# Shifting the rescaled high words in SBUF, and a second PSUM buffer for the early attention of a fused attention and feed-forward kernel

## Chip, cores and metric

One core of one Trainium2 chip runs the whole program. The metric is the device time of one execution in microseconds; the kernel before takes 642.7 us (median of 3 runs, 642.09 to 643.06).

## What is computed

The reference is chunked attention (batch 4, 8 heads, 768 positions of width 64; each chunk of 32 queries sees 16 keys to its left, itself, 8 to its right and 8 memory keys), whose output, 3072 tokens of width 512, goes through a feed-forward layer with a rational activation. The weights `w_in` and `w_out` come as float64.

```
scores = scale * q_c @ k_full.T;  a = exp(scores - max);  a = a / (sum(a) + 1e-9);  out_c = a @ v_full
x = out.reshape(3072, 512);  h = x @ w_in                                  # 512 x 2048
P = a0 + a1*h + a2*h^2 + a3*h^3;  Q = 1 + |b0|*|h| + |b1|*h^2
g = P / (Q + 1e-6);  result = g @ w_out                                     # 2048 x 512
```

## The kernel before, in words

The tokens form 8 blocks of 384. A block needs 4 units of attention (two heads each) and then 16 steps, one for each slice of 128 columns of `w_in`: 128 steps in all. In a step TensorE (PE) makes `h` with 12 matmuls (`g1`, L397), the activation chain turns `h` into `g` on ScalarE (ACT), VectorE (DVE) and GpSimd (POOL) (`chain_...`, L448 to L491), and a step or two later 9 matmuls add `g @ w_out` into three PSUM banks (`g2`, L412). Each operand is split into a high and a low float32r part, so every product is three matmuls.

A unit of attention is scores (`att_scores`, L274, PE), maximum and subtraction (`att_max`, L282 to L295, DVE), exponential (L300, ACT), transposes (`att_turn`, L315, PE), a copy (`att_keep`, L322, ACT), values (`att_values`, L331, PE), division (`att_norm`, L339 to L349, DVE), transposes back (`att_back`, L360, PE) and the split into `x_hi` and `x_lo` (L364 to L377). Scores, transposes, values and transposes back each take a fresh PSUM tile from `pa()` (L249 to L256).

The 32 halves of the weight slices are converted from float64 bits on the chip, each 128x512 words, in five steps: load the pair of 32-bit words to `w_raw` in SBUF (SP queue, L117); `w_abs` (L165, ACT) rescales the high word, read at a step of two words, with Prelu into a PSUM tile `stage`; `w_bits` (DVE) shifts `stage` left by 3 in place (L170) and ors it to the low word shifted right by 29 (L171), back into the low words of `w_raw`; `w_hi` (L179, ACT) rounds to the high part and `w_lo` (L184, POOL) subtracts it.

The first 30 steps, their attention and all conversions stand in an order written out by hand, the table `SEQ` (tokens `A`, `B`, `H`, `L` are `w_abs`, `w_bits`, `w_hi`, `w_lo`; `b01` is the scores of block 0, unit 1, `g` and `o` are `g1` and `g2`, `r` is `chain_ratio`). Each engine runs its instructions strictly in that order, and so does the SP queue with the loads. From step 30 on a loop sets the order, and `stage` is no longer used.

PSUM has 8 banks here: three for `o`, two for `h`, one for `cr` (the chain's reciprocal), and two in `ps_a`. While `SEQ` runs, the two of `ps_a` have the tags `pa0` and `pa1`, one buffer each: attention of blocks 1 and 2 always uses `pa0`; `stage` alternates between both for the first 6 conversions (`STAGE2`) and then uses `pa1`. Block 0 uses the banks of `o` and `cr`.

Of the kernel before, what the change touches and what calls it, by code (L numbers as in the profile page):

```python
# [12 lines left out]
F32 = mybir.dt.float32  # L13
F32R = mybir.dt.float32r
U32 = mybir.dt.uint32
AF = mybir.ActivationFunctionType
ALU = mybir.AluOpType
# [7 lines left out]
F64_REBIAS = 2.0 ** -111  # L25
SIGN_STEP = 2.0 ** 32
# [14 lines left out]
STAGE2 = 6  # L41
# [24 lines left out]
def attn_moe(ctx, tc, qk, vm, w, a, b, out):  # L66
    nc = tc.nc
    P = 128
    NBLK, NPAIR = qk.shape[:2]
    NJT, DM = w.shape[0], out.shape[1]  # L70
# [18 lines left out]
    ps_h = ctx.enter_context(tc.tile_pool(name="ps_h", bufs=2, space=bass.MemoryType.PSUM))  # L89
    ps_r = ctx.enter_context(tc.tile_pool(name="ps_r", bufs=1, space=bass.MemoryType.PSUM))  # L90
    hand_pool = ExitStack()
    ps_a = hand_pool.enter_context(tc.tile_pool(name="ps_a", bufs=1, space=bass.MemoryType.PSUM))

    nc.scalar.preload_act_table_set("natural_log_exp_and_others")

# [16 lines left out]
    def pin(ins):  # L112
        if pinned[0]:
            tc.keep_in_program_order(ins)
# [7 lines left out]
    conv, raws, split = {}, {}, {}  # L122
# [29 lines left out]
    def words(key):  # L152
        t = half(raws[key[1]], key[0]).rearrange("p (f two) -> p f two", two=2)
        return t[:, :, 0], t[:, :, 1]
# [6 lines left out]

    def w_abs(key):
        low, high = words(key)
        f = conv[key] = ps_a.tile([P, DM], F32, name="stage", tag=f"pa{int(done['A'] >= STAGE2 or done['A'] % 2)}")
        pin(nc.scalar.activation(f, high.bitcast(F32), AF.Prelu, scale=F64_REBIAS, alpha=-SIGN_STEP))  # L165

    def w_bits(key):
        low, high = words(key)
        fi = conv.pop(key).bitcast(U32)
        pin(nc.vector.tensor_scalar(fi, fi, 3, None, op0=ALU.logical_shift_left))  # L170
        pin(nc.vector.scalar_tensor_tensor(low, low, 29, fi, op0=ALU.logical_shift_right, op1=ALU.bitwise_or))  # L171

    def w_hi(key):
        kind, j = key
# [73 lines left out]
    turn, ring = [0], [False]  # L248

    def pa(i):  # L250
        turn[0] = (turn[0] + 1) % 4
        if i == 0:
            if turn[0] == 3:
                return ps_r.tile([P, 512], F32, name="pa", tag="cr")
            return ps_o.tile([P, DM], F32, name="pa", tag=f"o{turn[0]}")
        return ps_a.tile([P, 512], F32, name="pa", tag="pa" if ring[0] else "pa0")  # L256

    def places(i):
        return [(g, j, 4 * g + j if i < BLOCKWISE else NG * j + g) for g in range(NG) for j in range(4)]
# [8 lines left out]
    def att_scores(i, p):  # L268
        u = unit[i, p]
        users[qk_slot(i, p)] = users.get(qk_slot(i, p), 0) - 1  # L270
        s = u["s"] = pa(i)
        sv = s[:, :NG * 2 * KEYS].rearrange("x (g h w) -> x g h w", g=NG, h=2)
        for g, j, c in places(i):
            pin(nc.tensor.matmul(sv[j * CHUNK:(j + 1) * CHUNK, g], lhsT=u["q"][c],  # L274
                                 rhs=u["k"][c], start=True, stop=True, tile_position=(0, j * CHUNK)))
# [31 lines left out]
    def att_turn(i, p):  # L307
        u = unit[i, p]
        if i >= BLOCKWISE:
            u["eT"] = across(turn_blocks(u.pop("e").rearrange("x g w h -> x g (w h)")), "eT")  # L310
            return
        ep = u["ep"] = pa(i)
        e = u.pop("e")
        for g in range(NG):
            pin(nc.tensor.transpose(out=ep[:, g * P:(g + 1) * P], in_=e[:, g], identity=ident))  # L315
# [8 lines left out]
    def att_values(i, p):  # L324
        u = unit[i, p]
        if i == 0 and p >= 2:
            users[V_SLOTS[p - 2]] -= 1
        o = u["o"] = pa(i)
        ov = o[:, :NG * 2 * (D + 1)].rearrange("x (g h d) -> x g h d", g=NG, h=2)
        for g, j, c in places(i):  # L330
            pin(nc.tensor.matmul(ov[j * CHUNK:(j + 1) * CHUNK, g],  # L331
                                 lhsT=u["eT"][:, c * CHUNK:(c + 1) * CHUNK], rhs=u["v"][c],
                                 start=True, stop=True, tile_position=(0, j * CHUNK)))
# [166 lines left out]
    done = dict.fromkeys("wABHL", 0)  # L500
# [61 lines left out]

    single = dict(g=g1, s=chain_abs, p=chain_below, i=chain_line, j=chain_above, t=chain_inverse, r=chain_ratio, u=chain_hi, y=chain_lo, o=g2)
    convert = dict(w=lambda key: w_load(*key), A=w_abs, B=w_bits, H=w_hi, L=w_lo)

    def hand(token):
# [28 lines left out]
    ps_a = ctx.enter_context(tc.tile_pool(name="ps_b", bufs=2, space=bass.MemoryType.PSUM))  # L595
# [90 lines left out]
```

## Time and profile before

| what | value |
|---|---|
| time, median of 3 runs | 642.7 us (642.09 to 643.06) |
| profiled execution: span from first to last instruction | 641.9 us |
| around the span, against the median | 0.8 us |
| TensorE busy | 615.4 us, 96% |
| VectorE busy | 500.8 us, 78% |
| ScalarE busy | 432.7 us, 67% |
| GpSimd busy | 431.7 us, 67% |
| mean granted TensorE clock | 0.981 |

The trace has no time of its own for the execution beside its span, so the span stands for it; the lowest run (642.09) is 0.2 us above it. The table averages over stages with different limits: the slices of the page show TensorE near full from the fourth slice on, and all conversions lie in the first 178 us.

### The profile page before, as it was taken

The numbers are of one execution on the slowest core, as the hardware profiler recorded it, in microseconds if no ns is written. First come the engines' busy times: TensorE is split into PE (matmuls) and PEld (weight loads), VectorE is DVE, ScalarE is ACT, GpSimd is POOL, SyncE is SP. The second block draws the span as 40 slices with busy tenths as digits, with TensorE's granted clock in tenths as the row PEclk, the third lists the DMA queues.
The fourth block names the chain that finished last, engine by engine and source line by source line (L and its number), as shares of the span: only waits on it lengthen the run. The fifth ranks groups of instructions, "written<-read, shape, count | busy, mean of one in ns | idle before, by whom it ended". The sixth has DMA issues, their size and how long they took to land.

```text
span 641.9 us, 12300 instructions
## 1 busy us (share of the span) xinstructions
PE 615.4 (96%) x4312; PEld 537.7 (84%) x4312; DVE 500.8 (78%) x1001; ACT 432.7 (67%) x814; POOL 431.7 (67%) x457
## 2 busy tenths in 40 slices
PE   4769999999999999999999999999999999999997
PEld 3567787889988888888898888888988888999995
DVE  5777998997967878888787777887877787666665
ACT  4567787877965566665666766676666766676664
POOL 5457775868885656766666666676666666777762
PEclk8778999999999999999999999999999999999999
DMA  7998127403212385424322433214223310000001
GB/s 250 348 384 304 64 63 240 160 1 112 96 62 87 85 267 164 147 79 126 95 77 80 137 87 87 66 50 129 76 80 87 100 26 13 13 34 17 1 1 50
DMA packets 43566, 69.69 MB, mean 109 GB/s; under 512 B 26480, under 2 KB 26480, under 8 KB 43120
## 3 DMA queue, kind: packets, MB, share of 16 engines
q1 hardware_dynamic: 42256, 64.17, 31.5%
q10 hardware_dynamic: 960, 3.16, 1.5%
q0 software_dynamic: 288, 1.57, 0.8%
q8 instruction: 34, 0.56, 0.4%
q14 instruction: 28, 0.23, 0.1%
HBM read 51.58 MB, written 9.44 MB: 95 GB/s over the span
## 4 chain that ended last, share of the span: by engine, by line
PE 55%; issue 15%; POOL 13%; DVE 8%; DMA 4%; ACT 4%; SPq 1%; POOLq 0%; DVEq 0%; ACTq 0%
PE h L397 25%; PE o L412 23%; POOL glo L491 5%; POOL ghi L484 5%; PE pa L274 3%; PE pa L331 3%; DMA qk<-in_qk_dram 2%; DMA w_raw<-in_w_dram 2%; DVE stage L170 1%; DVE ct L477 1%; POOL cy L458 1%; DVE w_raw L171 1%; DVE cr L478 1%; DVE ct L479 1%; SPq L117 1%
## 5 line engine op out<-in xcount | busy, mean ns | idle before, releaser
L397 PE MATMUL h<-x_hi,w_hl 128*128 128x384 f32 x1024 | 268.5, 343 | 3.3 <-DVE ct L468 3.2
L412 PE MATMUL o<-w_hl,ghi 128*128 128x512 f32 x768 | 240.1, 393 | 0.3 <-ACT ghi L486 0.3
L458 POOL TENSOR_TENSOR cy<-cy,ha 128x384 f32<-128x384 f32 x128 | 130.3, 1018 | 148.4 <-ACT cy L454 146.1
L397 PEld LDWEIGHTS h<-x_hi,w_hl 128*128 128x128 f32 x1024 | 187.3, 190 | 17.3 <-issue 5.8
L397 PE MATMUL h<-x_lo,w_hl 128*128 128x384 f32 x512 | 173.8, 339 | 0.0
L412 PEld LDWEIGHTS o<-w_hl,ghi 128*128 128x128 f32 x768 | 141.5, 188 | 21.6 <-issue 1.0
L412 PE MATMUL o<-w_hl,glo 128*128 128x512 f32 x384 | 151.4, 394 | 0.4 <-POOL glo L491 0.2
L491 POOL TENSOR_TENSOR glo<-ct,ghi 128x384 fp32r<-128x384 f32 x126 | 127.9, 1015 | 9.1
L453 ACT ACTIVATE ha<-h 128x384 f32<-128x384 f32 x128 | 62.9, 492 | 100.9 <-PE h L397 96.2
L467 DVE TENSOR_TENSOR ct<-ct,h 128x384 f32<-128x384 f32 x128 | 70.1, 547 | 61.5 <-ACT ct L463 61.5
L484 POOL TENSOR_TENSOR ghi<-ct,zero 128x384 fp32r<-128x384 f32 x126 | 104.6, 830 | 9.8 <-DVE ct L479 7.3
L477 DVE SCALAR_TENSOR_TENSOR ct<-ct,par,cr 128x384 f32<-128x384 f32 x128 | 78.4, 612 | 37.1 <-ACT cr L473 34.0
L472 ACT ACTIVATE cr<-cy 128x384 f32<-128x384 f32 x128 | 63.3, 494 | 57.4 <-POOL cy L458 52.4
L397 PEld LDWEIGHTS h<-x_lo,w_hl 128*128 128x128 f32 x512 | 97.2, 190 | 0.0
L454 ACT ACTIVATE cy<-ha,bab 128x384 f32<-128x384 f32 x128 | 90.8, 710 | 4.2
L412 PEld LDWEIGHTS o<-w_hl,glo 128*128 128x128 f32 x384 | 72.0, 187 | 21.5 <-POOL glo L491 1.2
L463 ACT ACTIVATE ct<-h,par 128x384 f32<-128x384 f32 x128 | 84.0, 657 | 0.0
L468 DVE SCALAR_TENSOR_TENSOR ct<-ct,par,h 128x384 f32<-128x384 f32 x128 | 78.7, 615 | 4.5
L479 DVE SCALAR_TENSOR_TENSOR ct<-cr,ct 128x384 f32<-128x384 f32 x128 | 71.3, 557 | 4.4
L478 DVE SCALAR_TENSOR_TENSOR cr<-cy,cr 128x384 f32<-128x384 f32 x128 | 71.0, 555 | 0.4
L473 ACT ACTIVATE cr<-cr 128x384 f32<-128x384 f32 x128 | 60.8, 475 | 4.0
L184 POOL TENSOR_TENSOR w_hl<-w_raw,w_hl 128x512 fp32r<-128x512 f32 x32 | 42.0, 1311 | 26.0 <-ACT w_hl L179 25.0
(60 smaller groups left out, 419.9 us busy)
## 6 DMA issues: line engine op xcount, KB each, us to landing
qk<-in_qk_dram SPq DMA_DIRECT2D x56, 288.0 KB, 3.4
w_raw<-in_w_dram SPq DMA_DIRECT2D x26, 512.0 KB, 7.5
v_main<-in_vm_dram SPq DMA_DIRECT2D x56, 195.0 KB, 3.9
out_dram<-stage SPq DMA_DIRECT2D x24, 256.0 KB, 3.3
eT<-blocks SPq DMA_DIRECT2D x80, 48.0 KB, 2.0
xf<-blocks SPq DMA_DIRECT2D x80, 48.0 KB, 2.0
w_raw<-in_w_dram SPq DMA_DIRECT2D x3, 1024.0 KB, 4.7
qk<-in_qk_dram ACTq DMA_DIRECT2D x8, 288.0 KB, 3.6
```

Source lines behind the costliest of these rows:

```text
L397: pin(nc.tensor.matmul(h[:, :TB], lhsT=wt[:, cols], rhs=xt[i][:, ct, :], start=m == 0, stop=m == last))
L412: ins = nc.tensor.matmul(o, lhsT=gt[:, cols], rhs=wt, start=begin and m == 0, stop=end and m == 2)
L454: pin(nc.scalar.activation(c["y"], c["ha"], AF.Identity, scale=B1, bias=B0))
L458: pin(nc.gpsimd.tensor_tensor(c["y"], c["y"], c.pop("ha"), op=ALU.mult))
L463: pin(nc.scalar.activation(c["t"], c["h"], AF.Identity, scale=A3, bias=A2))
L467: pin(nc.vector.tensor_tensor(t, t, h, op=ALU.mult))
L468: pin(nc.vector.scalar_tensor_tensor(t, t, A1, h, op0=ALU.add, op1=ALU.mult))
L477: pin(nc.vector.scalar_tensor_tensor(t, t, A0, r, op0=ALU.add, op1=ALU.mult))
L478: pin(nc.vector.scalar_tensor_tensor(r, yy, QC, r, op0=ALU.add, op1=ALU.mult))
L479: pin(nc.vector.scalar_tensor_tensor(t, r, 2.0, t, op0=ALU.subtract, op1=ALU.mult, reverse0=True))
L484: pin(nc.gpsimd.tensor_tensor(ghi, chain[z]["t"], zero.broadcast_to([P, TB]), op=ALU.add))
L491: pin(engine.tensor_tensor(glo, chain.pop(z)["t"], gh[z].bitcast(F32), op=ALU.subtract))
```

## The change

`w_abs` writes the rescaled high word back to where it read it, in SBUF. `w_bits` shifts it there, and the or takes both of its inputs from SBUF. No `stage` tile is left, so `ps_a` becomes one tag `pa` with two buffers, and attention of blocks 1 and 2 in the first 30 steps alternates between two banks. Below the edit all lines move up by one.

```diff
-    ps_a = hand_pool.enter_context(tc.tile_pool(name="ps_a", bufs=1, space=bass.MemoryType.PSUM))
+    ps_a = hand_pool.enter_context(tc.tile_pool(name="ps_a", bufs=2, space=bass.MemoryType.PSUM))
...
     def w_abs(key):
         low, high = words(key)
-        f = conv[key] = ps_a.tile([P, DM], F32, name="stage", tag=f"pa{int(done['A'] >= STAGE2 or done['A'] % 2)}")
-        pin(nc.scalar.activation(f, high.bitcast(F32), AF.Prelu, scale=F64_REBIAS, alpha=-SIGN_STEP))
+        high = high.bitcast(F32)
+        pin(nc.scalar.activation(high, high, AF.Prelu, scale=F64_REBIAS, alpha=-SIGN_STEP))
 
     def w_bits(key):
         low, high = words(key)
-        fi = conv.pop(key).bitcast(U32)
-        pin(nc.vector.tensor_scalar(fi, fi, 3, None, op0=ALU.logical_shift_left))
-        pin(nc.vector.scalar_tensor_tensor(low, low, 29, fi, op0=ALU.logical_shift_right, op1=ALU.bitwise_or))
+        pin(nc.vector.tensor_scalar(high, high, 3, None, op0=ALU.logical_shift_left))
+        pin(nc.vector.scalar_tensor_tensor(low, low, 29, high, op0=ALU.logical_shift_right, op1=ALU.bitwise_or))
...
-        return ps_a.tile([P, 512], F32, name="pa", tag="pa" if ring[0] else "pa0")
+        return ps_a.tile([P, 512], F32, name="pa", tag="pa")
```

On PE, DVE, ACT and POOL the same instructions stand in the same order as before; what differs is their operands and what they wait for. On DVE, the first two conversions between steps of the chain (`w_raw` is the loaded weights, `stage` the PSUM tile, `ct` and `cr` tiles of the chain), before:

```order
L468 SCALAR_TENSOR_TENSOR ct<-ct,par,h 128x384 [waits DVE_49]
L170 TENSOR_SCALAR stage<-stage 128x512 [waits Activation_49]
L171 SCALAR_TENSOR_TENSOR w_raw<-w_raw,stage 128x512 [waits DMAHW1_49,DMAHW5_49,DVE_49,Pool_49]
L477 SCALAR_TENSOR_TENSOR ct<-ct,par,cr 128x384
L478 SCALAR_TENSOR_TENSOR cr<-cy,cr 128x384 [waits Pool_49]
```

and of the change:

```order
L467 SCALAR_TENSOR_TENSOR ct<-ct,par,h 128x384 [waits DVE_49]
L169 TENSOR_SCALAR w_raw<-w_raw 128x512 [waits DMAHW1_49,DMAHW5_49,Activation_49,Pool_49]
L170 SCALAR_TENSOR_TENSOR w_raw<-w_raw 128x512 [waits DVE_49]
L476 SCALAR_TENSOR_TENSOR ct<-ct,par,cr 128x384
L477 SCALAR_TENSOR_TENSOR cr<-cy,cr 128x384 [waits Pool_49]
```

Nothing moved; both instructions of a conversion now work on `w_raw` in SBUF alone.

On PE, the scores of the first two units of block 1 (`pa` is the attention's PSUM tile), ahead of the first step's `h`, before:

```order
L274 MATMUL pa<-qk 32x128 [waits DMAHW2_49,DMAHW1_49,DVE_49]
L360 MATMUL pa<-ident,xt 128x128 [waits DVE_49,Activation_49]
L274 MATMUL pa<-qk 32x128 [waits DMAHW5_49,DMAHW6_49,DVE_49,PE_49]
L397 MATMUL h<-x_hi_102,w_hl 128x384
...
L315 MATMUL pa<-ident,e 128x128 [waits DVE_49,PE_49]
```

and of the change:

```order
L273 MATMUL pa<-qk 32x128 [waits DMAHW2_49,DMAHW1_49]
L359 MATMUL pa<-ident,xt 128x128 [waits DVE_49,Activation_49]
L273 MATMUL pa<-qk 32x128 [waits DMAHW6_49,DMAHW5_49]
L396 MATMUL h<-x_hi_102,w_hl 128x384
...
L314 MATMUL pa<-ident,e 128x128 [waits PE_49]
```

The waits on DVE for a free bank are gone from these three.

On the SP queue one pair of loads of values (`v_main`, two of 195 KB) moves ahead of two loads of weights:

```order
 L117 DMA v_main_101<-in_vm_dram 64x780 x2
 L117 DMA w_raw<-in_w_dram 128x1024 x2
-L117 DMA w_raw<-in_w_dram 128x2048 x2
+L117 DMA w_raw<-in_w_dram 128x2048
+L117 DMA v_main_101<-in_vm_dram 64x780 x2
+L117 DMA w_raw<-in_w_dram 128x2048
 L117 DMA part_109<-spare 128x512 x3
 L117 DMA w_raw<-in_w_dram 128x2048
-L117 DMA v_main_101<-in_vm_dram 64x780 x2
 L117 DMA qk<-in_qk_dram 64x1152 x2
```

The second whole-slice load of weights now stands behind the load of `v_main_101`.

## Rows read from the trace of the kernel before

**Rows 1.** The page's first line and its part 1: busy time, share of the span, instructions of an engine.

```profile
span 641.9 us, 12300 instructions
PE 615.4 (96%) x4312; PEld 537.7 (84%) x4312; DVE 500.8 (78%) x1001; ACT 432.7 (67%) x814; POOL 431.7 (67%) x457
```

**Rows 2.** Busy time by stretch. Columns: stretch, its length, busy time and number of instructions of PE, PEld, DVE, ACT, POOL, then the granted TensorE clock, the share of the DMA engines and GB/s.

```profile
10.00:37.50 27.50, 19.39 (x271) 13.94 (x272) 18.42 (x42) 13.84 (x28) 11.70 (x10) 0.69 0.97 336
...
45.60:53.00 7.40, 7.35 (x28) 7.32 (x29) 5.23 (x9) 3.21 (x6) 5.22 (x5) 0.61 1.02 417
53.00:87.00 34.00, 30.60 (x271) 24.52 (x269) 31.86 (x63) 28.35 (x55) 24.51 (x25) 1.00 0.40 132
87.00:146.00 59.00, 58.10 (x434) 49.47 (x435) 53.35 (x107) 47.39 (x92) 44.16 (x45) 1.00 0.36 116
146.00:191.00 45.00, 44.89 (x227) 40.50 (x225) 34.88 (x63) 34.65 (x66) 38.48 (x40) 1.00 0.28 96
191.00:641.90 450.90, 446.25 (x3022) 394.33 (x3022) 346.59 (x703) 293.04 (x549) 295.32 (x315) 1.00 0.28 80
```

**Rows 3.** Pieces of the chain that ended last, in order of time: start, length, what.

```profile
30.92 6.52 DMA w_raw<-in_w_dram
...
37.52 0.64 ACT stage L165
...
45.65 7.06 PE h L397 x24
...
87.00 2.37 PE h L397 x12
...
132.37 4.20 PE h L397 x24
```

**Rows 4.** The same chain summed by line, first from 56.6 to 87 us, then from 146.3 to 191.1 us.

```profile
by line: DVE stage L170 15.9%; DVE w_raw L171 15.9%; issue 14.0%; DVE ct L467 9.6%; DVE ct L477 8.6%; DVE cr L478 8.2%; DVE ct L479 7.3%; DVE mx L287 5.6%; DVE ct L468 4.6%; DVE xt L343 3.7%; DVE x_lo L377 3.3%; DVE e L291 2.1%; DVE rinv L3
...
by line: issue 13.8%; POOL w_hl L184 11.7%; POOL glo L491 9.1%; POOL ghi L484 7.5%; POOL cy L458 6.7%; DVE ct L477 6.4%; DVE cr L478 5.4%; DVE ct L479 5.4%; DVE w_raw L171 4.6%; DVE stage L170 4.5%; ACT spare L431 3.3%; ACT cr L473 3.2%; DV
```

**Rows 5.** From the timeline of PE: start, length, instructions, and in brackets the idle time before and what ended it.

```profile
34.08 1.35 PE L274 MATMUL pa<-qk 128*32 128x128 f32 x24 [2.10 <-DVE e L291]
...
43.88 0.52 PE L315 MATMUL pa<-ident,e 128*128 128x128 f32 x3 [1.20 <-DVE xt L343]
...
45.65 1.01 PE L397 MATMUL h<-x_hi,w_hl 128*128 128x384 f32 x2 [1.25 <-DVE ct L468]
```

**Rows 6.** Groups of instructions by line: count, busy us and mean ns of one, idle time before and what ended it.

```profile
L165 ACT ACTIVATE stage<-w_raw 128x512 f32<-128x512 f32 x32 | 20.4, 636 | 11.8 <-DMA w_raw<-in_w_dram 10.8 <-DVE w_raw L171 1.0
L179 ACT CAST w_hl<-w_raw 128x512 fp32r<-128x512 f32 x32 | 21.0, 656 | 2.7 <-DVE w_raw L171 2.6
L170 DVE TENSOR_SCALAR stage<-stage 128x512 uint32<-128x512 uint32 x32 | 22.2, 692 | 7.3 <-ACT stage L165 7.3
L211 DVE MEMSET qk<- 128x768 f32 x4 | 2.8, 698 | 1.3 <-PEq L678 1.0
L491 DVE TENSOR_TENSOR glo<-ct,ghi 128x384 fp32r<-128x384 f32 x2 | 1.1, 556 | 0.6 <-ACT ghi L486 0.6
L467 DVE TENSOR_TENSOR ct<-ct,h 128x384 f32<-128x384 f32 x128 | 70.1, 547 | 61.5 <-ACT ct L463 61.5
```

**Rows 7.** All 32 instructions of L171: shortest, median and longest in ns, first and last start in us.

```profile
L171 DVE SCALAR_TENSOR_TENSOR w_raw<-w_raw,stage x32: 687/689/706, 8.8 to 176.3; 128x512 uint32<-128x512 uint32 x32
```

**Rows 8.** From the timelines of DVE and of POOL: the seven L171 between 57 and 87 us, and then the POOL instructions that run when six of them start (start and length in us).

```profile
57.91 0.69 DVE L171 SCALAR_TENSOR_TENSOR w_raw<-w_raw,stage 128x512 uint32<-128x512 uint32 x1
62.18 0.69 DVE L171 SCALAR_TENSOR_TENSOR w_raw<-w_raw,stage 128x512 uint32<-128x512 uint32 x1
68.77 0.69 DVE L171 SCALAR_TENSOR_TENSOR w_raw<-w_raw,stage 128x512 uint32<-128x512 uint32 x1
72.67 0.69 DVE L171 SCALAR_TENSOR_TENSOR w_raw<-w_raw,stage 128x512 uint32<-128x512 uint32 x1
75.58 0.70 DVE L171 SCALAR_TENSOR_TENSOR w_raw<-w_raw,stage 128x512 uint32<-128x512 uint32 x1
80.97 0.69 DVE L171 SCALAR_TENSOR_TENSOR w_raw<-w_raw,stage 128x512 uint32<-128x512 uint32 x1
83.56 0.69 DVE L171 SCALAR_TENSOR_TENSOR w_raw<-w_raw,stage 128x512 uint32<-128x512 uint32 x1
...
57.72 1.02 POOL L458 TENSOR_TENSOR cy<-cy,ha 128x384 f32<-128x384 f32 x1
62.13 1.02 POOL L491 TENSOR_TENSOR glo<-ct,ghi 128x384 fp32r<-128x384 f32 x1
68.42 1.02 POOL L491 TENSOR_TENSOR glo<-ct,ghi 128x384 fp32r<-128x384 f32 x1
75.45 0.82 POOL L484 TENSOR_TENSOR ghi<-ct,zero 128x384 fp32r<-128x384 f32 x1
80.35 1.01 POOL L491 TENSOR_TENSOR glo<-ct,ghi 128x384 fp32r<-128x384 f32 x1
82.97 1.32 POOL L184 TENSOR_TENSOR w_hl<-w_raw,w_hl 128x512 fp32r<-128x512 f32 x1 [0.64 <-DVE e L291]
```

**Rows 9.** From the timeline of the SP queue: the loads of whole weight slices around the place where `v_main_101` moves (start, issue time).

```profile
119.14 0.33 SPq L117 DMA_DIRECT2D w_raw<-in_w_dram  x1
153.11 0.33 SPq L117 DMA_DIRECT2D w_raw<-in_w_dram  x1
```

## The prediction, made before the changed kernel was run

> **What bounds the kernel now.** The page first: TensorE is busy for 615.4 of 641.9 us [rows 1]. So a change to conversions can matter only where TensorE waits. The busy times by stretch say where that is: after 191 us it is busy 446.25 of 450.9 us, and nothing is converted there any more; from 87 to 191 us it is busy nearly throughout (58.10 of 59 and 44.89 of 45) [rows 2]. The loss is before 87 us.
>
> The chain says why. From 30.92 us it runs through a load of weights, DMA engines being 97% busy, to its landing at 37.5; there ScalarE, which had waited in its queue for it, begins a long run of work [rows 2, 3]. At 45.65 the chain passes to TensorE: 24 matmuls take 7.06 us, since the granted clock of the stretch is 0.61, between the levels of 1.2 and 2.4 GHz; the same 24 take 4.20 us at full clock [rows 2, 3]. From about 53 to 87.00 the chain is **VectorE**: busy for 31.86 of 34 us, with TensorE idle for 3.4 [rows 2, 3]. The two instructions of the conversion carry 15.9% each of the chain from 56.6 to 87 us, 4.8 us each, seven of either [rows 4, 8]. After 87 TensorE leads, but from 146 to 191 us it has company: the chain there goes through POOL, DVE and ACT, POOL is busy for 38.48 of 45 us, and TensorE has 0.1 us of idle time [rows 2, 4]. What lengthens that chain lengthens the run.
>
> **The change, part by part.**
>
> *The freed bank.* It removes waits of attention for a free PSUM tile. The two long ones are 2.10 us at 34.08 (for DVE's subtraction) and 1.20 us at 43.88 [rows 5]. I count both at nothing. The first is followed by matmuls whose results ScalarE reads only after the load that landed at 37.5 [rows 3]; the cover is that load. Behind the second TensorE waits again, 1.25 us, for DVE to free a bank of `h` [rows 5], which the change leaves as it is. If both covers were gone, 3.3 us would be saved, and at most 2.9 more (7.06 less 4.20) if TensorE then came to its 24 matmuls at full clock. Neither wait lies on the chain, so I take the low end.
>
> *Prelu into SBUF.* ACT wrote 512 elements to PSUM in 636 ns; from and to SBUF the nearest row takes 656 [rows 6]: 0.02 us each, 0.6 for all 32, of which I take five as lying on the chain, 0.1 us. A step of two words on the write could cost more; a doubling of those five would be 3.2 us. But VectorE writes with that step at no visible price (L171, 0.69 us like L170) [rows 6, 7], so 0.1 stands.
>
> *The shift in SBUF.* 692 ns in PSUM. The nearest rows in SBUF: L171 itself, 689 ns with one input and the output there, which gives no change; and the fill of 768 elements in 698 ns, 0.91 ns each, which for 512 would be 0.47 us, a gain of 0.22 [rows 6, 7]. With one input it is nearest to L171: 0.
>
> *The or with both inputs in SBUF.* This is the term that decides. Before, one input was in PSUM, and all 32 took 687 to 706 ns, though POOL worked beside 24.51 of 34 us [rows 2, 7]. A DVE instruction with two SBUF tensors occurs only at the end, with POOL done: 556 ns against 547 for one with a PSUM input [rows 6]. So the trace shows the price with POOL idle (nothing) and not the price with POOL reading SBUF. Low end: nothing. High end: the two engines exclude each other. Then the or waits for the POOL instruction that is running, and POOL's next one waits for the or. I walk along the seven [rows 8]: at 57.91 POOL runs until 58.74, a wait of 0.83; at 62.18 until 63.15, 0.97; 68.77 until 69.44, 0.67; at 72.67 nothing runs; 75.58 until 76.27, 0.69; 80.97 until 81.36, 0.39; 83.56 until 84.29, 0.73. Sum **4.3 us**, all on DVE, on the chain [rows 4].
>
> From 146 to 191 us POOL is busy 38.48 of 45 us with 40 instructions of 0.96, so an or meets one with a chance of 0.86 and waits half of it, 0.41. The chain's share of L171 there, 4.6% of 44.8 us, is three of them [rows 4]: **1.2 us**. Two more conversions fall where POOL itself is the chain; they put its next instruction off by the or's 0.69 us each [rows 7]: **1.4 us**. Between 87 and 146 us DVE has 5.7 us to spare [rows 2], which hides the rest. What queues behind the waiting or is the chain's own DVE work, which frees `h` for TensorE and feeds POOL; no wait is left that could take this in.
>
> I take the high end of this mechanism, 4.3 + 1.2 + 1.4 = 6.9 us, because six of seven starts fall into a running POOL instruction and nothing I see in the rows would let two engines that both stream SBUF tensors pass for free at all of them. The row to weigh against is L171's steadiness, and it has one SBUF input, not two.
>
> The Trainium skill, SBUF — State Buffer, section Who interferes with whom, speaks against this change: a VectorE instruction with two SBUF inputs contends with a GpSimd instruction that reads SBUF, and whichever starts first keeps the other out for its whole length. By that rule the sum is the 6.9 us above; by L171's row alone it is 0. No row here shows the case.
>
> *The moved load.* The pair of `v_main_101` loads goes ahead of the weights that SP issues at 153.11. Between 119.14 and then SP issues nothing [rows 9], the buffer's last reader on TensorE is earlier, and DMA is 28% busy there [rows 2]; the 1.1 us of issue fit in. Nothing.
>
> **Sum.** 6.9 + 0.1 = 7.0 us on the profiled 641.9, to 648.9. That execution is 0.8 us below the median of the runs, so I expect **649.7 us**.
>
> **Rivals.**
>
> *Both instructions collide, by turns.* The shift too waits, and POOL takes its turn between shift and or, so that the or waits for a whole instruction. For: POOL has work ready most of the time. From 53 to 87 us it is busy 0.72 of the time with instructions of 0.98 us [rows 2]: the shift waits 0.35, the or 0.98 in six of seven; 2.5 + 5.9 = 8.4 us. From 146 to 191, three shifts of 0.41 and three ors of 0.96, 4.1 us, and POOL is put off by both instructions twice, 2.8. Sum 15.3, 657.9 us or a little below, since a longer stretch leaves POOL idler. Against: the shift has one input.
>
> The Trainium skill, VectorE: DVE Perf Modes, section The perf-mode tier table, gives a float32 `tensor_scalar` within SBUF the double rate; an estimate from it is 0.42 us for this shift. Within the rival before, ten shifts on the chain would give back 2.7 us, 655.2; without collisions the seven before 87 us would give 1.9 us. No run here shows it.
>
> *No collision, and a shorter shift (the faster side).* If the engines share SBUF freely and the shift runs at the rate of the fill, seven of 0.22 us leave the chain before 87: 1.5 us, where TensorE's 3.4 us of idle time can take it; after 146 TensorE is full, nothing more [rows 2, 6]. 642.7 - 1.5 = 641.2. It decides if the or takes no more than 0.72 us beside POOL: at 0.75 the seven ors have eaten a third of the gain, and what is left is within 0.2%. With the 3.3 us of the bank's two waits on top, 637.9, which I hold unlikely.
>
> *No effect.* The or is as steady as L171 is now and the shift takes its 0.69 us: only Prelu's 0.1 is left, 642.8. For: the same instructions stand in the same order. Against: both DVE instructions get other operands.
>
> **Chances.** A measurement of this kernel can tell about 0.2%, 1.3 us, from no change. The gain is bounded by a few tenths per conversion, the loss by a POOL instruction of 0.8 to 1.3 us, and VectorE leads the chain. Collision of the or: 0.42. By turns: 0.21. No effect: 0.16. Faster: 0.21. So slower 0.63, same 0.16, faster 0.21. The range reaches from the faster rival's side, 640.5, to 656.0 in the rival by turns; the likeliest case's own range is 646 to 653, from half of its waits to some waits of the shift.
>
> **What would show it.** Right: the ors before 87 us take 0.7 to 1.7 us, or stand behind gaps that end with a POOL instruction; POOL's instructions at those places are stretched or late; L165 at about 0.65 us; TensorE's wait for DVE before 87 us grows by some 4 us, and idle time appears between 146 and 191 us; the waits at 34 and 44 us are gone and the 24 matmuls still begin near 45.65. Wrong: ors at 0.69 us beside a busy POOL; a shift well under 0.69 with nobody late; or a start of those matmuls before 45 us or at a higher clock, which would mean that the bank was worth what I counted at nothing.

## The result, and the profile after

The changed kernel takes **651.38 us** (median of 4 runs, 650.53 to 652.73) against 642.55 for the kernel before on the same chip (4 runs): a ratio of 1.0138, 95% interval 1.0124 to 1.0153, or 8.9 us more (8.0 to 9.8). The forecast was 649.7. The profiled execution has a span of 649.7 us; its own time was 651.43, so 1.7 us lie around the span, and 1.7 to 1.8 in every later run. The 0.8 us taken for that before were therefore too little: the traced execution of the kernel before probably took about 643.6 us, 1 us above its median.

The first line and part 1 of its page, beside [rows 1]:

```profile
span 649.7 us, 12292 instructions
PE 614.7 (95%) x4312; PEld 535.2 (82%) x4312; DVE 517.6 (80%) x1001; ACT 434.2 (67%) x814; POOL 442.2 (68%) x457
```

TensorE has as much to do as before (614.7 us against 615.4), in a longer span. VectorE is busy 16.8 us longer and GpSimd 10.5, with the same 1001 and 457 instructions. Busy time by stretch, columns as in [rows 2]:

```profile
45.60:53.00 7.40, 7.40 (x30) 7.29 (x31) 5.61 (x9) 3.53 (x8) 5.48 (x5) 0.67 1.01 413
53.00:87.00 34.00, 28.50 (x243) 23.34 (x242) 32.41 (x57) 26.52 (x51) 26.11 (x23) 1.00 0.38 123
87.00:146.00 59.00, 56.30 (x445) 47.36 (x445) 56.71 (x106) 46.31 (x89) 44.34 (x43) 1.00 0.37 122
146.00:191.00 45.00, 42.79 (x211) 37.22 (x210) 40.83 (x63) 33.83 (x63) 39.88 (x38) 1.00 0.21 75
191.00:649.70 458.70, 453.22 (x3054) 399.91 (x3054) 350.25 (x709) 297.43 (x557) 300.52 (x320) 1.00 0.27 80
```

The granted clock is 1.00 from 53 us on, as before, so the loss is waiting: TensorE is idle for 5.5 us before 87 (3.4 before the change), 2.7 up to 146 (0.9) and 2.2 up to 191 (0.1). The groups by line, beside [rows 6, 7] (`w_abs` L165, the shift L169, the or L170, then three of GpSimd's four lines, and these three again before the change):

```profile
L165 ACT ACTIVATE w_raw<-w_raw 128x512 f32<-128x512 f32 x32 | 21.8, 681 | 7.8 <-DMA w_raw<-in_w_dram 7.8
L169 DVE TENSOR_SCALAR w_raw<-w_raw 128x512 uint32<-128x512 uint32 x32 | 24.1, 753 | 3.2 <-ACT w_raw L165 3.2
L170 DVE SCALAR_TENSOR_TENSOR w_raw<-w_raw 128x512 uint32<-128x512 uint32 x32 | 37.4, 1170 | 1.1
L457 POOL TENSOR_TENSOR cy<-cy,ha 128x384 f32<-128x384 f32 x128 | 135.5, 1058 | 144.0 <-ACT cy L453 141.7 <-DVE xt L348 2.3
L490 POOL TENSOR_TENSOR glo<-ct,ghi 128x384 fp32r<-128x384 f32 x126 | 130.5, 1036 | 9.1
L183 POOL TENSOR_TENSOR w_hl<-w_raw,w_hl 128x512 fp32r<-128x512 f32 x32 | 44.0, 1374 | 22.7 <-ACT w_hl L178 22.6
...
L458 POOL TENSOR_TENSOR cy<-cy,ha 128x384 f32<-128x384 f32 x128 | 130.3, 1018 | 148.4 <-ACT cy L454 146.1 <-DVE xt L349 2.3
L491 POOL TENSOR_TENSOR glo<-ct,ghi 128x384 fp32r<-128x384 f32 x126 | 127.9, 1015 | 9.1
L184 POOL TENSOR_TENSOR w_hl<-w_raw,w_hl 128x512 fp32r<-128x512 f32 x32 | 42.0, 1311 | 26.0 <-ACT w_hl L179 25.0 <-DVE e L291 0.6
```

The or takes 1170 ns on average, not 687 to 706. The shift takes 753 on average, which mixes two kinds. How both come about is in the timelines of DVE and of POOL; first a conversion beside GpSimd, then the one at 73.68 us, where nothing runs on GpSimd between 73.61 and 75.61:

```profile
56.71 0.85 DVE L169 TENSOR_SCALAR w_raw<-w_raw 128x512 uint32<-128x512 uint32 x1
57.60 1.39 DVE L170 SCALAR_TENSOR_TENSOR w_raw<-w_raw 128x512 uint32<-128x512 uint32 x1
...
73.68 0.42 DVE L169 TENSOR_SCALAR w_raw<-w_raw 128x512 uint32<-128x512 uint32 x1
74.14 0.69 DVE L170 SCALAR_TENSOR_TENSOR w_raw<-w_raw 128x512 uint32<-128x512 uint32 x1
```

```profile
56.45 0.82 POOL L483 TENSOR_TENSOR ghi<-ct,zero 128x384 fp32r<-128x384 f32 x1
57.24 1.20 POOL L457 TENSOR_TENSOR cy<-cy,ha 128x384 f32<-128x384 f32 x1
58.39 1.46 POOL L490 TENSOR_TENSOR glo<-ct,ghi 128x384 fp32r<-128x384 f32 x1
...
72.28 1.33 POOL L183 TENSOR_TENSOR w_hl<-w_raw,w_hl 128x512 fp32r<-128x512 f32 x1
75.61 1.31 POOL L183 TENSOR_TENSOR w_hl<-w_raw,w_hl 128x512 fp32r<-128x512 f32 x1 [2.00 <-ACT w_hl L178]
```

The two engines go **by turns**, and a wait is inside the duration of the instruction that waits. `ghi`, the first, keeps its 0.82 us and ends at 57.27; the shift, begun during it, ends at 57.56. `cy`, begun at 57.24 during the shift, ends at 58.44, 0.88 behind the shift. The or ends at 58.99, 0.55 behind `cy`; `glo` at 59.85, 0.86 behind the or. With GpSimd idle the shift takes 0.42 us and the or 0.69.

The chain summed by line, from 56.6 to 90.2 us and from 146.3 to 198.5, beside [rows 4]:

```profile
by line: DVE w_raw L170 24.2%; DVE w_raw L169 15.2%; issue 11.1%; DVE ct L466 7.3%; DVE ct L478 6.6%; DVE ct L476 6.2%; DVE cr L477 6.0%; DVE mx L286 5.1%; DVE ct L467 4.0%; DVE xt L342 3.3%; DVE x_lo L376 2.8%; ACT w_hl L178 2.0%; DVE e L2
...
by line: DVE w_raw L170 10.6%; issue 7.5%; DVE w_raw L169 7.4%; DVE ct L478 6.5%; DVE ct L476 6.4%; POOL cy L457 6.4%; DVE cr L477 5.6%; ACT cy L453 5.5%; POOL w_hl L183 5.0%; POOL ghi L483 4.9%; PE h L396 4.5%; POOL glo L490 4.2%; DVE ct L
```

In the first stretch the two carry 39% of 33.6 us, 13.2 us, against 9.7 before; in the second 18% of 52.2 us, 9.4 us, against 4.1. Where TensorE waits, from its timeline, beside [rows 3, 5]:

```profile
32.18 0.86 PE L273 MATMUL pa<-qk 128*32 128x128 f32 x24 [0.35 <-DMA qk<-in_qk_dram]
...
41.68 0.87 PE L330 MATMUL pa<-v_main,eT 128*32 128x130 f32 x24 [3.02 <-ACT eT L321]
...
45.52 1.01 PE L396 MATMUL h<-x_hi,w_hl 128*128 128x384 f32 x2 [2.49 <-DVE ct L467]
...
90.15 0.62 PE L396 MATMUL h<-x_hi,w_hl 128*128 128x384 f32 x2 [1.69 <-DVE ct L467]
```

The waits for a bank at 34 and 44 us are gone, and waits of 3.02 and 2.49 us stand in their place: the 24 matmuls begin at 45.52 instead of 45.65. The matmuls of `h` that began at 87.00 begin at 90.15.

To say where time goes I compare the start of the same VectorE instruction in two traces; the difference is called the lag. The changed kernel is ahead by 0.48 us at 56.1, behind by 3.98 at 93.9, 3.96 at 134.8 and 8.27 at 180.4, and by 7.4 from 191 us on. So against this trace it loses about 4.5 us before 94, nothing up to 135, and about 3.4 net behind that. The table of lags behind the experiments divides this more finely, against a kernel without the collision: the first of the eight middle conversions lies before 94, and from 90 to 141 us 1.1 us are lost. That gave the theory, *by turns for both*, and the experiments test it, each stage, and the bank.

### The profile page after: what moved, and what is told of

It reads as the page before. It is cut to its first block, busy times and chain, and to the rows that moved or that the text cites. A ratio compares the mean times of both kernels' runs of the same rounds, so it can differ in the third digit from the quotient of the medians.

```text
span 649.7 us, 12292 instructions
## 1 busy us (share of the span) xinstructions
PE 614.7 (95%) x4312; PEld 535.2 (82%) x4312; DVE 517.6 (80%) x1001; ACT 434.2 (67%) x814; POOL 442.2 (68%) x457
## 4 chain that ended last, share of the span: by engine, by line
PE 49%; DVE 15%; issue 13%; POOL 11%; DMA 5%; ACT 4%; SPq 1%; POOLq 0%; DVEq 0%; ACTq 0%
PE h L396 23%; PE o L411 21%; POOL glo L490 5%; POOL ghi L483 4%; DVE w_raw L170 3%; DMA w_raw<-in_w_dram 3%; PE pa L330 2%; PE pa L273 2%; DVE w_raw L169 2%; DVE ct L476 2%; DVE ct L478 2%; DVE cr L477 2%; DVE ct L466 1%; SPq L117 1%; DMA v_main<-in_vm_dram 1%
## 5 line engine op out<-in xcount | busy, mean ns | idle before, releaser
L457 POOL TENSOR_TENSOR cy<-cy,ha 128x384 f32<-128x384 f32 x128 | 135.5, 1058 | 144.0 <-ACT cy L453 141.7
L490 POOL TENSOR_TENSOR glo<-ct,ghi 128x384 fp32r<-128x384 f32 x126 | 130.5, 1036 | 9.1
L476 DVE SCALAR_TENSOR_TENSOR ct<-ct,par,cr 128x384 f32<-128x384 f32 x128 | 78.4, 612 | 36.5 <-ACT cr L472 33.6
L183 POOL TENSOR_TENSOR w_hl<-w_raw,w_hl 128x512 fp32r<-128x512 f32 x32 | 44.0, 1374 | 22.7 <-ACT w_hl L178 22.6
```

What stands on the lines that cost most here:

```text
L457: pin(nc.gpsimd.tensor_tensor(c["y"], c["y"], c.pop("ha"), op=ALU.mult))
L476: pin(nc.vector.scalar_tensor_tensor(t, t, A0, r, op0=ALU.add, op1=ALU.mult))
L490: pin(engine.tensor_tensor(glo, chain.pop(z)["t"], gh[z].bitcast(F32), op=ALU.subtract))
```

## Experiments

Microseconds beside ratios are the ratio less one, times 642.55; every ratio is to the kernel before on the same chip.

**1. The collision by itself** (m1_turns). This kernel leaves out all of the reference's work. Stretches of 12 instructions, alone and side by side:

```diff
+    beside(lambda i: nc.vector.scalar_tensor_tensor(low, low, 29, high, **OR),
+           lambda i: nc.gpsimd.tensor_tensor(pc[i % 2], c1, c2, op=ALU.subtract))
+    beside(lambda i: nc.vector.tensor_scalar(high, high, 3, None, op0=SH),
+           lambda i: nc.gpsimd.tensor_tensor(pc[i % 2], c1, c2, op=ALU.subtract))
...
```

> Computes nothing of the reference (its output is zeros): stretches of 12 instructions of each kind by themselves and beside each other, apart from the rest, with the conversion's operands on VectorE and 128x384 tiles on GpSimd. By turns: alone, the or in SBUF 0.69 us, the shift in SBUF 0.42, the shift from SBUF to PSUM 0.69, GpSimd's subtraction 1.0. Beside the subtraction, a pair of or and subtraction takes the sum, 1.7 us, and a pair of shift in SBUF and subtraction 1.4; the shift to PSUM and the or with one PSUM input keep their own time and the subtraction its 1.0. The prediction's theory: the same for the or, but shift in SBUF and subtraction run side by side, 1.0 us a pair. Rival, SBUF bandwidth is shared instead of taken by turns: each is stretched while both run, but a pair takes less than the sum, 1.2 us or so. Beside a fill on GpSimd, which reads nothing, the or keeps its 0.69 us if the two engines share only the way in (the Trainium skill, SBUF — State Buffer, section Who interferes with whom, has it so), and takes the sum if they share the way out as well.

From the timeline of all engines (`raw` is in SBUF and `stage` in PSUM; rows that start within 0.15 us of each other ran side by side):

```profile
4.75 8.69 DVE L101 SCALAR_TENSOR_TENSOR raw<-raw 128x512 uint32<-128x512 uint32 x12 [2.76 <-SPq L88]
13.59 5.52 DVE L102 TENSOR_SCALAR raw<-raw 128x512 uint32<-128x512 uint32 x12
19.26 8.72 DVE L103 TENSOR_SCALAR stage<-raw 128x512 uint32<-128x512 uint32 x12 [0.15 <-SPq L88]
28.17 11.45 POOL L104 TENSOR_TENSOR pc<-c,c 128x384 f32<-128x384 f32 x12 [26.67 <-SPq L88]
39.71 16.09 DVE L105 SCALAR_TENSOR_TENSOR raw<-raw 128x512 uint32<-128x512 uint32 x12 [11.73 <-SPq L88]
39.82 16.83 POOL L106 TENSOR_TENSOR pc<-c,c 128x384 f32<-128x384 f32 x12 [0.19 <-SPq L88]
56.80 12.90 DVE L107 TENSOR_SCALAR raw<-raw 128x512 uint32<-128x512 uint32 x12 [1.00 <-SPq L88]
56.84 13.71 POOL L108 TENSOR_TENSOR pc<-c,c 128x384 f32<-128x384 f32 x12 [0.19 <-SPq L88]
70.69 8.72 DVE L109 TENSOR_SCALAR stage<-raw 128x512 uint32<-128x512 uint32 x12 [1.00 <-SPq L88]
70.73 11.51 POOL L110 TENSOR_TENSOR pc<-c,c 128x384 f32<-128x384 f32 x12 [0.19 <-SPq L88]
82.39 8.64 DVE L111 SCALAR_TENSOR_TENSOR raw<-raw,stage 128x512 uint32<-128x512 uint32 x12 [2.98 <-SPq L88]
82.43 11.54 POOL L112 TENSOR_TENSOR pc<-c,c 128x384 f32<-128x384 f32 x12 [0.19 <-SPq L88]
94.12 9.77 DVE L113 SCALAR_TENSOR_TENSOR raw<-raw 128x512 uint32<-128x512 uint32 x12 [3.09 <-SPq L88]
94.19 16.63 POOL L114 TENSOR_SCALAR pc<-c 128x384 f32<-128x384 f32 x12 [0.22 <-SPq L88]
110.97 8.70 DVE L115 SCALAR_TENSOR_TENSOR raw<-raw 128x512 uint32<-128x512 uint32 x12 [7.08 <-SPq L88]
110.98 4.38 POOL L116 MEMSET pc<- 128x384 f32 x12 [0.17 <-SPq L88]
```

Per instruction in a row of 12: alone, the or 0.72 us, the shift 0.46, GpSimd's subtraction 0.95. Or and subtraction 1.40 a pair (the sum would be 1.68), shift and subtraction 1.14 (1.41). Both pairs are far above the 0.95 of running side by side, so the shift collides as the or does: the prediction's theory falls there. Both pairs are 0.27 below the sum, which is less than my theory expected. By the totals alone two engines that share a bandwidth would fit as well. The single instructions at the start of or and subtraction decide it, and with them one summary of the GpSimd instruction with one input (count, then shortest, median and longest in ns):

```profile
39.71 0.69 DVE L105 SCALAR_TENSOR_TENSOR raw<-raw 128x512 uint32<-128x512 uint32 x1 [11.73 <-SPq L88]
39.82 1.43 POOL L106 TENSOR_TENSOR pc<-c,c 128x384 f32<-128x384 f32 x1 [0.19 <-SPq L88]
40.43 1.37 DVE L105 SCALAR_TENSOR_TENSOR raw<-raw 128x512 uint32<-128x512 uint32 x1
...
L114 POOL TENSOR_SCALAR pc<-c x12: 1165/1412/1663, 94.2 to 109.7; 128x384 f32<-128x384 f32 x12
```

The first or has a subtraction beside it for 0.58 of its 0.69 us and is no longer than alone; a shared bandwidth would have stretched it. The subtraction ends 0.85 us behind the or (0.99 is its length alone), the second or 0.55 behind the subtraction (0.69 alone). So they go by turns, and whoever waits ends 0.14 us sooner than its own length would give, twice in a pair. The timeline of the changed kernel above shows the same, by 0.13 to 0.16. With a PSUM output or a PSUM input nobody waits (8.72 and 8.64; 11.51 and 11.54). A GpSimd instruction with one SBUF input collides too: beside the ors it takes 1.66 us, behind the last of them 1.17, and every second or takes 0.87. Beside a fill nobody waits (8.70 us).

The Trainium skill, SBUF — State Buffer, section Who interferes with whom, says which pairs contend: it lets GpSimd contend with VectorE instructions with two SBUF inputs and with those that run at double rate, the shift among them, and not by writes alone beside an or. The trace agrees (1.40 and 1.14 us a pair, and 8.70 us for the ors beside a fill); only "fully blocks" for the whole length is 0.27 us a pair too dear.

**2. The conversions back, but through SBUF first** (e3_shift_to_psum).

```diff
-        f = conv[key] = ps_a.tile([P, DM], F32, name="stage", tag=f"pa{int(done['A'] >= STAGE2 or done['A'] % 2)}")
-        pin(nc.scalar.activation(f, high.bitcast(F32), AF.Prelu, scale=F64_REBIAS, alpha=-SIGN_STEP))
+        f = high.bitcast(F32)
+        pin(nc.scalar.activation(f, f, AF.Prelu, scale=F64_REBIAS, alpha=-SIGN_STEP))
...
+        fi = ps_a.tile([P, DM], F32, name="stage", tag=f"pa{int(done['B'] >= STAGE2 or done['B'] % 2)}").bitcast(U32)
+        pin(nc.vector.tensor_scalar(fi, high, 3, None, op0=ALU.logical_shift_left))
```

> The kernel before with one edit: Prelu writes in place in SBUF, and the shift reads SBUF and writes the PSUM tile, which the or then reads as before. No VectorE instruction has two SBUF inputs, and the shift has its output in PSUM. By turns: an instruction with one SBUF input and a PSUM output is not excluded, so the shift takes 0.69 to 0.70 us, the or 0.69, GpSimd's instructions 0.82 and 1.02 as before, and the time is that of the kernel before, 642 to 643.5 us (Prelu's 0.045 us more on the few that lie on the chain). Rival, any VectorE read of SBUF beside GpSimd waits, or SBUF words at a step of two are the trouble: the shift takes 0.8 us or more and the time rises to 645 us or more.

642.27 us, ratio 1.0004 (0.9992 to 1.0017). The groups of the shift and the or:

```profile
L170 DVE TENSOR_SCALAR stage<-w_raw 128x512 uint32<-128x512 uint32 x32 | 22.0, 688 | 7.0 <-ACT w_raw L165 7.0
L171 DVE SCALAR_TENSOR_TENSOR w_raw<-w_raw,stage 128x512 uint32<-128x512 uint32 x32 | 22.1, 690 | 1.2
```

As expected: with one operand of each instruction in PSUM the whole loss is gone, though the shift still reads SBUF. Prelu in SBUF (677 ns a piece here) costs nothing that can be seen.

**3. The or alone** (e2_or_alone). Prelu into `stage` as before, the shift from `stage` to SBUF:

```diff
-        pin(nc.vector.tensor_scalar(fi, fi, 3, None, op0=ALU.logical_shift_left))
-        pin(nc.vector.scalar_tensor_tensor(low, low, 29, fi, op0=ALU.logical_shift_right, op1=ALU.bitwise_or))
+        pin(nc.vector.tensor_scalar(high, fi, 3, None, op0=ALU.logical_shift_left))
+        pin(nc.vector.scalar_tensor_tensor(low, low, 29, high, op0=ALU.logical_shift_right, op1=ALU.bitwise_or))
```

> The kernel before with one edit: the shift reads the PSUM tile and writes its result to SBUF, so that the or has both inputs in SBUF and the shift has one in PSUM. This is the case that the prediction's sum describes. The prediction's theory (only an instruction with two SBUF inputs collides, and waits for the rest of a running GpSimd instruction): shift 0.69 us, or 1.0 to 1.2 us on average, 647.5 to 649.5 us. By turns for both: the same for this kernel, but then it must be faster than the changed one, since there the shift collides as well and lets a GpSimd instruction in between shift and or: 1 to 3 us below 651.4. Rival, the shift's collision costs nothing because its double rate pays for it: within 1 us of 651.4. Rival, SBUF operands cost nothing and the loss lies elsewhere: 642.5 us.

649.37 us, ratio 1.0123 (1.0102 to 1.0144), 7.9 us (6.6 to 9.3). The times don't tell it from the changed kernel; the traces do. Between 57 and 195 us this one loses 4.7 us, the changed kernel 8.3 (table of lags below). Why the times say more than the trace is left open; the execution that was traced took 648.79.

**4. One bank again** (e1_one_bank).

```diff
-    ps_a = hand_pool.enter_context(tc.tile_pool(name="ps_a", bufs=2, space=bass.MemoryType.PSUM))
+    ps_a = hand_pool.enter_context(tc.tile_pool(name="ps_a", bufs=1, space=bass.MemoryType.PSUM))
...
-        return ps_a.tile([P, 512], F32, name="pa", tag="pa")
+        return ps_a.tile([P, 512], F32, name="pa", tag="pa" if ring[0] else "pa0")
```

> The changed kernel with the bank taken back: attention of the first 30 steps has one PSUM buffer again, the second stays empty, and the conversions work in SBUF. By turns (VectorE and GpSimd exclude each other in SBUF, for the shift as for the or, and that is the whole loss): the bank was worth 0 to 0.5 us, so 651 to 652 us, and the seven conversions between 57 and 87 us again take 13.3 us for shift and or together. Rival, the bank or the order that it allows is part of the loss (attention that runs earlier takes TensorE at the wrong time): 649.5 us or less. Rival, the bank gave back something large that hides a larger loss: 653.5 us or more.

652.36 us, ratio 1.0169 (1.0145 to 1.0192), 10.9 us (9.3 to 12.3); one of its four runs has a granted clock of 0.939. Against the changed kernel's 8.9 the times leave room for a bank worth 2 us or more, while the trace shows none: 4.7 us are lost between 56 and 94 us and 4.4 between 135 and 180, against 4.5 and 4.3 in the changed kernel. The seven conversions take 12.8 us for shift and or, where 13.3 was expected. The bank was therefore tried without the collision:

**5. The bank without the SBUF or** (e6_short_ring): experiment 2 with `ps_a` and `pa()` as in the changed kernel and

```diff
+        fi = ps_a.tile([P, DM], F32, name="stage", tag="pa").bitcast(U32)
```

> A version that keeps the change's bank without its price: Prelu in place in SBUF, the shift from SBUF to a PSUM tile, and that tile, which now lives from the shift to the or only, takes its turn with attention's tiles in one ring of two PSUM buffers. Theory: the bank is worth next to nothing, since TensorE's waits at 34 and 44 us stood behind other waits: 641.5 to 643 us, no difference from before. Rival 1, the bank is worth what the medians of the changed kernel and of e1_one_bank differ by, 1 to 2 us: 640 to 641 us. Rival 2, the ring puts the shift behind attention's use of a bank: 643.5 us or more.

641.80 us, ratio 0.9996 (0.9984 to 1.0008), so -0.3 us (-1.0 to 0.5). TensorE's timeline at the 24 matmuls, first here and then in experiment 2:

```profile
44.72 1.01 PE L397 MATMUL h<-x_hi,w_hl 128*128 128x384 f32 x2 [2.49 <-DVE ct L468]
```

```profile
44.78 1.01 PE L397 MATMUL h<-x_hi,w_hl 128*128 128x384 f32 x2 [0.90 <-DVE ct L468]
```

With two buffers attention waits less, and TensorE then waits longer for VectorE's `ct` (2.49 us instead of 0.90). The second buffer, which attention shares with the conversions here, is worth nothing that the times show. This version doesn't beat the kernel before either.

**6. Stage by stage** (e7_early, e7_middle, e7_late): experiment 2, with shift and or in SBUF only in the first 18, the next 8 or the last 6 conversions.

```diff
-        fi = ps_a.tile([P, DM], F32, name="stage", tag=f"pa{int(done['B'] >= STAGE2 or done['B'] % 2)}").bitcast(U32)
+        fi = high
+        if not (done['B'] < 18):
+            fi = ps_a.tile([P, DM], F32, name="stage", tag=f"pa{int(done['B'] >= STAGE2 or done['B'] % 2)}").bitcast(U32)
```

> The kernel of e3 (the shift goes from SBUF to PSUM and one bank serves attention), but in the first 18 of the 32 conversions, those up to 87 us, the shift and the or work in SBUF as in the changed kernel. By turns, with the chain's owners as the trace of the changed kernel shows them (behind the kernel before by 4.4 us from 56 to 94 us): e3's 642.3 and 3.6 to 4.6 us, 646 to 647. Rival, TensorE makes it up between 87 and 191 us, where it waited little before: 643 to 644.5 us.

645.69 us, ratio 1.0054 (1.0039 to 1.0069): 3.5 us. Against experiment 2 the lag grows by 3.6 us between 54 and 92 us and then stays (4.65 to 4.66 us at 157, 178 and 205): TensorE makes nothing up. The time is just under the 646 to 647 that were expected.

> As e7_early, but the eight conversions between 87 and 146 us are the ones in SBUF. The prediction's step (VectorE's 5.7 us of spare time hide them): 642 to 643 us. Rival, eight waits of about 0.7 us and the stretched GpSimd instructions are more than VectorE has to spare, and VectorE becomes the chain from 115 us on: 644 to 645.5 us. In the changed kernel the lag grew by next to nothing in this stretch (3.98 us at 94, 3.96 at 135), but there TensorE's order was already held up.

642.08 us, ratio 1.0000 (0.9990 to 1.0011), so 0.0 us (-0.6 to 0.7): by the times nothing, as the prediction had it. But in the two traces the lag grows by 1.3 us, and in the changed kernel it grows by 1.1 over the same instructions. Which of the two holds is open.

> As e7_early, but the last six conversions, between 146 and 191 us, are the ones in SBUF. By turns: the changed kernel's lag grew by 3.4 to 4.3 us there, so 645.5 to 646.8 us. The prediction's sum for this stretch (2.6 us): 645 us. If the loss of the three stretches adds up, e7_early, e7_middle and e7_late are together 8 to 10 us above three times e3. Rival, the late loss is an echo of the early one (order and buffers upset before 146 us) and six conversions alone cost little: 643.5 us or less.

645.71 us, ratio 1.0057 (1.0040 to 1.0074): 3.7 us. The six conversions alone cost as much as the seven on the early chain; the lag grows by 3.4 us. The first of the six starts at 142.7 us in the kernel before. Together the three kernels are 6.7 us above three times experiment 2, where 8 to 10 were expected.

**7. Late, the or alone** (e8_late_or): in the last six conversions only, Prelu writes `stage` and the shift goes from there to SBUF, as in experiment 3.

```diff
+        if done['A'] >= 26:
+            f = conv[key] = ps_a.tile([P, DM], F32, name="stage", tag="pa1")
...
+        if key in conv:
+            fi, src = high, conv.pop(key).bitcast(U32)
```

> As e7_late, but in the last six conversions (146 to 191 us) only the or works in SBUF alone: Prelu writes a PSUM tile as in the kernel before, the shift reads it and writes SBUF. It splits the late loss of e7_late (3.4 us over e3) between shift and or. By turns for both, with the waits between them: without the shift no GpSimd instruction slips in between shift and or, ors of 0.9 to 1.25 us as e2_or_alone shows them there, and the lag grows by 1.3 us: 643 to 644 us. Rival, the or carries the late loss (the prediction's step, 2.6 us, in which the shift is free): 645 to 646 us.

645.08 us, ratio 1.0045 (1.0028 to 1.0063): 2.9 us, which is the rival's figure. But the lag grows by 1.5 us, as the theory had it. Groups of the six, here and then in e7_late:

```profile
L176 DVE SCALAR_TENSOR_TENSOR w_raw<-w_raw 128x512 uint32<-128x512 uint32 x6 | 6.0, 1000 | 0.2
L175 DVE TENSOR_SCALAR w_raw<-stage 128x512 uint32<-128x512 uint32 x6 | 4.1, 683 | 0.0
```

```profile
L173 DVE SCALAR_TENSOR_TENSOR w_raw<-w_raw 128x512 uint32<-128x512 uint32 x6 | 8.1, 1356 | 0.2
L172 DVE TENSOR_SCALAR w_raw<-w_raw 128x512 uint32<-128x512 uint32 x6 | 5.8, 961 | 0.0
```

Taking the shift out shortens the ors as well, from 1356 to 1000 ns: after a shift in SBUF a GpSimd instruction stands ready, and the or waits for all of it. How the late 3.7 us divide is left open: the or alone is 1.5 by the trace, 2.9 (1.8 to 4.1) by the times, and the traced execution, 643.24 us, is the fastest of the six by 1.8. The two kernels also differ in one load: e7_late has the moved pair of `v_main`, at 136.97 us, and e8_late_or does not.

**8. The changed kernel again** (r_after).

> The changed kernel again, unedited, beside e8_late_or and the kernel before on one chip, for the sum of the stages: e7_early, e7_middle and e7_late stand 3.3, -0.3 and 3.3 us from the kernel before, 6.3 us together. If the stages add up, 648 to 650 us. If the early lag makes the middle dear (VectorE's spare time is used up there), 651 to 652.5 us, as the first runs of it gave.

648.87 us (5 runs, 648.77 to 651.10), ratio 1.0114 (1.0094 to 1.0135): 7.3 us, where the three stages give 3.5 + 0 + 3.7 = 7.2. By these times the stages add up, within about 2 us: the five runs fall into two groups, three at 648.8 and two at 650.7 and 651.1, the first runs gave 8.9, and the traced execution is one of the upper group.

VectorE's time in shift and or together, summed from the timelines (us):

| conversions | 11, to 56 us | 7, to 87 | 8, to 141 | 6, from 142 |
|---|---|---|---|---|
| before | 15.2 | 9.7 | 11.1 | 8.3 |
| changed | 18.7 | 13.3 | 15.5 | 14.1 |
| or alone (e2) | 19.3 | 12.3 | 14.1 | 10.3 |
| the stage alone (e7) | | 12.9 | 15.0 | 13.9 |
| cost to the run (e7) | | 3.5 | 0 | 3.7 |

The first 11 have no cell in the last row: e7_early holds them too. Its growth behind 54 us (3.6) is as large as its cost (3.5), so they are given nothing, but this is not shown to better than 1 us.

How much the lag against experiment 2 grows, in us; the stretches are counted in the kernel before, each trace is one execution, and the last row has each of the three kernels' growth from 57 to 195 us:

| lag grows by | 57 to 90 us | 90 to 141 | 141 to 195 | sum |
|---|---|---|---|---|
| kernel before | 0.0 | 0.4 | 0.0 | 0.4 |
| e6_short_ring | 0.0 | 0.1 | 0.0 | 0.1 |
| changed | 3.6 | 1.1 | 3.5 | 8.3 |
| changed again (r_after) | 3.7 | 1.3 | 3.5 | 8.5 |
| one bank (e1) | 3.7 | 1.4 | 3.5 | 8.6 |
| or alone (e2) | 2.7 | 0.7 | 1.4 | 4.7 |
| the stage alone (e7) | 3.5 | 1.3 | 3.5 | 8.4 |

In the traces too the stages add up, to 8.4 us, and the middle one is not free there. That lies between the two measurements of the changed kernel, 8.9 and 7.3.

## Why the prediction came out as it did

- *Where the loss is* was right in the main: before 87 us and from 142 on, nothing behind 195. Between, the times show nothing and the traces 1.1 to 1.3 us.
- *The or with both inputs in SBUF* was right in its mechanism. Its waits before 87 us were forecast at 4.3 us and measured 8.13 - 4.82 = 3.3 in the changed kernel, and 7.54 - 4.82 = 2.7 in e2_or_alone, the case that the sum describes. The walk charged the whole rest of the running instruction, while 0.13 us or more of each wait is saved at its end; that is some 0.8 us of the difference, and the rest was not followed up.
- **The step that failed: the shift at nothing.** It collides as well (1.14 us a pair), and alone it runs at 0.42 us, not at the 0.69 of the row that I put it beside. Before 87 us the two nearly cancel: seven shifts take 5.14 us, 4.84 before. So 4.3 for the one stood for 3.6 for both, which is luck. The rival by turns had the mechanism, and the double rate in a separate sentence; its 15.3 us let every wait count in full and the shift stay at 0.69.
- *87 to 146 us, hidden by VectorE's 5.7 us to spare*: right by the times (0.0 us, -0.6 to 0.7). The eight conversions took 4.4 us more, and in the traces 1.1 to 1.3 of it lengthens the run, so the cover may not have been whole.
- **146 to 191 us, 2.6 us, was mis-sized**: 3.7 by the times (2.6 to 4.8), 3.5 by the traces. I took three ors on the chain at half a GpSimd instruction each and two that put GpSimd off, five in all. The sixth starts at 142.7 us, where I held it hidden, and with it the lag of e7_late grows by 1.3 us. VectorE had 10.1 us to spare there [rows 2], more than in the stretch before, and it was no cover: shift and or took 14.1 us instead of 8.3, and 9.4 instead of 4.1 on the chain. My reason, that GpSimd's `ghi` waits for VectorE's `ct` and `ct` stands behind shift and or, is argued and not shown: `ghi` waits for `ct` in the stretch before as well. Three shifts of 1.4 to 1.5 us, which the forecast had at 0.69, are part of it.
- *The freed bank at nothing*: right, and for the reason given: behind the waits for a bank TensorE waits for `ct` anyway (2.49 us instead of 0.90).
- *Prelu, 0.1 us*: 0.045 us an instruction instead of 0.02, and 0.3 us (-0.5 to 1.1) in experiment 2: too small to see. *The moved load, nothing*: the pair of `v_main` loads now issues at 143.39 us, the lone weight load behind it at 158.55, and ScalarE's waits for weights from 84 to 190 us are 2.1 us, 3.5 before. No run tried it alone. It moved in e1_one_bank, e7_late and r_after too, but no engine waits for a load between 146 and 191 us, in the changed kernel or in e7_late.
- The sum, 7.0, stands against 8.9 in the first runs, 7.3 in the second and 8.3 to 8.5 in their traces. By the traces the early term was 0.7 us too high and the middle and late ones 1.1 and 0.9 too low, so that the sum came as close as it did is partly luck.

## What to carry to other kernels

In this kernel, freeing PSUM by moving a VectorE instruction's operands to SBUF was not free beside GpSimd: the or with two SBUF inputs and the shift from SBUF to SBUF take turns with a GpSimd subtraction that reads SBUF, at 1.40 and 1.14 us a pair, 0.27 less than the sum of both. One operand in PSUM avoids it; a scratch tile that lives from the shift to the or is enough, and it can share a ring with other users. Spare time of an engine is not cover by itself: with 5.7 us to spare VectorE took eight collisions for nothing by the times (1.3 us by the trace), and with 10.1 us six cost 3.7. What tells them apart was not tested; where two engines feed each other, follow who waits for whom.

## What was not expected of the hardware

- A wait by turns shows nowhere as idle time: it lies within the duration of the waiting instruction. The or's group has 1.1 us of idle time and 15 us more of busy time. A mean duration that changes though the instruction's size does not is the sign.
- A shift of words at a step of two within SBUF is faster than one into PSUM (0.46 us a piece in a row of 12, against 0.73), so the instruction that the change moved became shorter alone and yet dearer in the kernel (753 ns on average, 692 before).
- The first 50 us differ from one execution to the next: from 10 to 37.5 us the granted clock was 0.69 in the kernel before, 1.00 in experiment 2 and 0.81 in e7_late, and the VectorE instruction that starts at 56.7 us in the kernel before came 1.8 us sooner in experiment 2 and 2.7 sooner in e7_late. The clock of that stretch alone does not order them, and the distance stays: 2.2 us at the end for experiment 2. So distances between two later points of a trace were used beside the medians.
